# Loading token tile 1 in two halves on two queues, and moving one statistic ahead of an apply

## The chip, the cores and the metric

The kernel runs on one core of one Trainium2 chip. Its time is the device time of one execution in microseconds (us). The core has five engines that run side by side, each with its own list of instructions in a fixed order: TensorE (PE in the profile) multiplies matrices, VectorE (DVE), ScalarE (ACT) and GpSimd (POOL) work on elements, and SyncE (SP) issues most of the transfers between device memory and the on-chip memory. ScalarE issues a few transfers too. An engine waits on semaphores that others raise; matmul results go to PSUM, which has eight banks, and from there they are copied out.

## The reference

One input x of 2048 tokens by 640 features is normalised over its features (mean and variance, no scale), and the result goes through two branches that are added to x:

```
xn = layernorm(x)
A:  q, k, v = split(xn @ wqkv)                # 32 heads of 20
    phi(u) = [softmax(u @ w_phi), softmax(-(u @ w_phi))]   per head
    kv = phi(k)^T v ;  z = sum over tokens of phi(k)
    o = (phi(q) kv) / (phi(q) z + 1e-6)
    a = o @ wo
B:  b = (silu(xn @ w1) * (xn @ w3)) @ w2      # 640 -> 1536 -> 640
out = x + a + b
```

All tensors in memory are bfloat16.

## The kernel before

The 2048 tokens are 16 tiles of 128. Each tile of x is loaded with tokens on partitions (`x_tok`), normalised there, and transposed to features on partitions (`xnT`), 5 chunks of 128 features. Tiles 0 to 3 are transposed by TensorE (`xn_transpose`, L514), tiles 4 to 15 by transposing transfers. From `xnT` TensorE computes v (`v_part`, L559: five matmuls of 512 columns and five of 128 for a tile), the folded k and q projections, and the gated block (`mlp`, L681) in blocks of 512 tokens, so that the first gated block needs all of tiles 0 to 3.

The whole program is built by a list scheduler in Python. `P.op` and `P.dma` describe an operation with its reads, writes and an assumed cost; about a dozen generators (`norms`, `transposes`, `attention`, `mlps` and others, from L735) each yield their next step; the loop at L943 takes the step that, by the assumed costs, can start first, with ties broken by the generators' order. `commit` (L172) books it on its engine. For a load, `commit` adds its bytes, over an assumed rate, to one common bus, and takes a completion time from that. Afterwards `emit` (L212) turns the booked order into one instruction list for each engine, with waits where a dependency crosses engines. So a change in one step can change the order of later ones.

The start of the program is in `first_loads` (L414) and `norms` (L735). `first_loads` issues the loads in this order. On SP: the first half of tile 0 (columns 0 to 319), tile 1, tile 2, the last 128 columns of the v weights `wv`, tile 3, the first third of w1 and w3, `phi_s`, and later ones. On ScalarE's queue: the second half of tile 0, chunks 0 to 2 of the first 512 columns of `wv`, then chunks 3 and 4. The first v matmuls of a tile take chunk 0, 1, 2, 3, 4 in this order.

`norms` orders the normalisation. Tiles 0, 2 and 3 get their statistics on VectorE: two instructions, one for each half of the features (`ln_half`, L455), an aggregate, and a power on GpSimd for the reciprocal standard deviation (`ln_rstd`, L459); then `ln_apply` (L493) normalises the tile in place on VectorE. Tile 1's statistics are taken by ScalarE instead: `act_sum` (L470) twice over the whole tile, a sum for the mean and a sum of squares, then `act_rstd` (L482) with one small VectorE instruction and one on GpSimd. ScalarE's list at the start is therefore: its transfers, the load of its function table and a warm-up, the two sums of tile 1, then its two copies of tile 0's transposes from PSUM to `xnT` (`PARTS`, L511), and so on. For tile 0, VectorE copies chunks 0 and 1, ScalarE chunks 2, 3 and 4.

`transposes` (L800) lets tile 1's transposes go only after the five wide v matmuls of tile 0; `norms` yields `ln_apply(2)` only after tile 1's transposes are booked. `attention` (L820) issues 39 warm-up matmuls, the v parts of tiles 0 to 3 with their copies out of PSUM by ScalarE (`v_store`, L563), and then the k and v projections. After tile 3 `norms` yields a VectorE memset of the ones that stand beside v in `v2` (L758), which v's copies of tiles 2 and 3 must follow, and `block_diag` (L523) on GpSimd, which waits for `phi_s`.

Of the kernel before, what the change touches and what calls it, by code (L numbers as in the profile page):

```python
# [3 lines left out]
ACT = mybir.ActivationFunctionType  # L4
# [5 lines left out]
D = 640  # L10
# [239 lines left out]
def bass_parallel_sum__linear_kernel_hedgehog__glu_gated_swiglu__prompt_kernel(  # L250
# [16 lines left out]
    P = _Program(nc)  # L267
# [12 lines left out]
    def new(name, shape, dtype, offset=None):  # L280
        size = mybir.dt.size(dtype)
        for n in shape[1:]:
            size *= n
        return P.sbuf(name, shape, dtype, region(size) if offset is None else offset)
# [22 lines left out]
    x_tok = new("x_tok", [128, T, D], bf, RX)  # L307
# [83 lines left out]
    def memset(eng, o, v):  # L391
        P.op(eng, "memset", [o], [], (o, v), cost=0.15 + free(o) / 960)
# [7 lines left out]
    x_t = A_x.rearrange("b (t p) d -> p (b t) d", p=128)  # L400
# [6 lines left out]
    def w13(a, b):  # L407
        P.dma("SP", w1_s[:, :, a:b], w1_t[:, :, a:b])
        P.dma("SP", w3_s[:, :, a:b], w3_t[:, :, a:b])

    def load_x(a, b):
        P.dma("SP", x_tok[:, a:b, :], x_t[:, a:b, :])

    def first_loads():  # L414
        def part_wv(eng, i, j, a, b):
            P.dma(eng, wv[:, i:j, a:b], wqkv_t[:, i:j, 2 * D + a:2 * D + b])

        P.dma("SP", x_tok[:, 0, 0:320], x_t[:, 0, 0:320])
        P.dma("ACT", x_tok[:, 0, 320:D], x_t[:, 0, 320:D])
        load_x(1, 2)  # L420
        load_x(2, 3)
        part_wv("ACT", 0, 3, 0, 512)
        part_wv("ACT", 3, DC, 0, 512)
        part_wv("SP", 0, DC, 512, D)
        load_x(3, 4)
        w13(0, 512)
        P.dma("SP", phi_s[:], phi_t)
        P.dma("SP", wqkT[:, DC:2 * DC, :], A_wqkv[:, D:2 * D], True)
        load_x(4, 8)
        load_x(8, 12)  # L430
        load_x(12, 16)
        P.dma("SP", wqkT[:, 0:DC, :], A_wqkv[:, 0:D], True)


    def consts():
        memset("DVE", t1[:, 2, 0:128], 0.0)
        memset("DVE", warm[:], 0.0)
        memset("DVE", bst[:, :, 12:14], 0.0)
        memset("DVE", bst[:, :, 14:15], D * EPS)
        act(warm[:], warm[:], ACT.Exp)  # L440
        memset("POOL", ident[:], 0.0)
        select(ident[:], 0, [[-1, 128]], 1, ALU.not_equal, 1.0)
        memset("POOL", GM[:], 1.0)
        select(GM[:], 0, [[128, DC], [-DH, H]], 1, ALU.is_ge, 0.0)
        select(GM[:], DH, [[-128, DC], [DH, H]], -1, ALU.is_gt, 0.0)
        memset("POOL", mhalf[:], -0.5)
        memset("POOL", M3[:, 0:3], 1.0)
        select(M3[:, 0:3], 0, [[-40, 3]], 1, ALU.is_ge, 0.0)
        select(M3[:, 0:3], 40, [[40, 3]], -1, ALU.is_gt, 0.0)
        memset("POOL", ekt[:, T * 2 * D:T * 2 * D + 48], 1.0)  # L450

    def v_heads(a):
        return a.rearrange("p (g x) -> p g x", x=64)[:, :, 0:63].rearrange("p g (h c) -> p g h c", c=21)

    def ln_half(t, q):  # L455
        i, o = x_tok[:, t, 320 * q:320 * q + 320], bst[:, t, 6 * q:6 * q + 6]
        P.op("DVE", "bn_stats", [o], [i], (o, i), cost=0.48)

    def ln_rstd(t0, n):  # L459
        for t in range(t0, t0 + n):  # L460
            o, i = mv[:, t, 0:2], bst[:, t, 0:15]
            P.op("DVE", "bn_aggr", [o], [i], (o, i), cost=0.22)
        m, v, r, z = mv[:, t0:t0 + n, 0], mv[:, t0:t0 + n, 1], rstd[:, t0:t0 + n, 0], rstd[:, t0:t0 + n, 1]
        P.op("POOL", "tensor_tensor", [r], [v, mhalf[:, 0:n]], (r, v, mhalf[:, 0:n], ALU.pow),
             cost=0.57 if t0 < 4 else 0.73)
        if t0 >= 4:
            P.op("POOL", "tensor_scalar_mul", [z], [m], (z, m, -1.0), cost=0.25)
            P.op("POOL", "tensor_tensor", [z], [z, r], (z, z, r, ALU.mult), cost=0.25)

    def act_sum(t, f, o, bias=None, scale=1.0):  # L470
        j = t1[:].rearrange("p n c -> p (n c)")[:, 0:D]
        i = x_tok[:, t, :]
        kw = dict(accum_out=o, scale=scale)
        if bias is not None:
            kw["bias"] = bias
        P.op("ACT", "activation", [j, o], [i] + ([] if bias is None else [bias]), (j, i, f), kw, cost=0.75)
# [5 lines left out]
    def act_rstd(t):  # L482
        scalar_op(t, rstd[:, t, 0:1], mv[:, t, 1:2], 1.0 / D, EPS)
        r = rstd[:, t, 0:1]
        P.op("POOL", "tensor_tensor", [r], [r, mhalf[:, 0:1]], (r, r, mhalf[:, 0:1], ALU.pow), cost=0.57)

    def ln_stats(t0, n):
        for t in range(t0, t0 + n):
            ln_half(t, 0)
            ln_half(t, 1)  # L490
        ln_rstd(t0, n)

    def ln_apply(t, a=0, b=D):  # L493
        o, m, s, z = x_tok[:, t, a:b], mv[:, t, 0:1], rstd[:, t, 0:1], rstd[:, t, 1:2]
        if t < 4 or P.free["DVE"] < P.free["ACT"] + 0.45:
            P.op("DVE", "tensor_scalar", [o], [o, m, s],
                 (o, o, m, s, ALU.add if t == 1 else ALU.subtract, ALU.mult),
                 cost=0.06 + (b - a) / 1880)
        else:
            P.op("ACT", "activation", [o], [o, s, z], (o, o, ACT.Identity), dict(bias=z, scale=s),  # L500
                 cost=0.9)
# [232 lines left out]

    def norms():  # L735
        yield lambda: (first_loads(), consts())
        yield lambda: act_sum(1, ACT.Copy, mv[:, 1, 0:1], scale=-1.0 / D)
        yield lambda: (ln_half(0, 0), ln_half(0, 1), ln_rstd(0, 1))
        yield lambda: act_sum(1, ACT.Square, mv[:, 1, 1:2], mv[:, 1, 0:1])
        yield lambda: (ln_apply(0, 0, 256), ln_apply(0, 256, D))  # L740
        done["ln"] = 1
        while done["t"] < 1:
            yield None
        yield lambda: act_rstd(1)
        yield lambda: (ln_half(2, 0), ln_half(2, 1))
        yield lambda: ln_apply(1)
        done["ln"] = 2
        yield lambda: ln_rstd(2, 1)
        while done["t"] < 2:
            yield None  # L750
        yield lambda: ln_apply(2)
        done["ln"] = 3
        yield lambda: (ln_half(3, 0), ln_half(3, 1), ln_rstd(3, 1))
        yield lambda: ln_apply(3)
        done["ln"] = 4
        while done["t"] < 4:
            yield None
        yield lambda: memset("DVE", v_heads(v2[:].rearrange("p t n -> p (t n)"))[:, :, :, DH], 1.0)  # L758
        yield block_diag
        done["bd"] = 1  # L760
        todo = []
        for t in range(4, T + 2, 2):
            if t == T or t > done["k"] + 8:
                for u in todo:
                    yield lambda u=u: ln_apply(u)
                    done["ln"] = u + 1
                todo = []
            if t == T:
                break
            while t > done["k"] + 8:  # L770
                yield None
            yield lambda t=t: ln_stats(t, 2)
            for u in todo:
                yield lambda u=u: ln_apply(u)
                done["ln"] = u + 1
            todo = [t, t + 1]
# [153 lines left out]
    def outs():  # L930
        for t in range(T):
            while done["o"] <= t or done["h"] <= t // 4:
# [4 lines left out]
    URGENT = {0: 4.0, 4: 4.0}  # L937
    PROMPT = (6, 8, 10, 11)
    streams = [norms(), transposes(), fold_k(), attention(), k_norms(), loads(), key_values(),
               q_toks(), q_norms(), queries(), q_transposes(), o_transposes(), mlps(), outs()]  # L940
    n = len(streams)
# [100 lines left out]
```

## Time and profile before

| what | us |
|---|---|
| median of 3 runs | 268.19 (268.18 to 268.28) |
| time of the profiled execution | 268.84 |
| its span | 267.1 |
| TensorE busy | 262.7 (98%) |
| VectorE busy | 167.2 (63%) |
| ScalarE busy | 100.8 (38%) |
| GpSimd busy | 99.2 (37%) |
| TensorE's share of the chain that ended last | 96% |

The span reaches from the first to the last instruction of the profiled execution; the execution's time has 1.7 us around it. The clock granted to TensorE is full in every slice of the page. A row of a timeline has the start in us from the span's start, the length of the group, the engine and line, the operation, and what is written from what, with shapes and a count; in brackets stands how long the engine was idle before it and what ended that. Nearly all operations have line 102, the helper that records them, so rows are told apart by their tiles. A matmul's end is modelled, so the starts say more than the lengths.

### The profile page before, as it was taken

To read this page: it belongs to the slowest core of one execution; us is meant where nothing else is said; L and a number is where in the kernel's file an instruction comes from. 1 tells how busy PE (TensorE), PEld (TensorE's weight loads), DVE (VectorE), ACT (ScalarE), POOL (GpSimd) and SP (SyncE) were. 2 spreads that over 40 slices of the span, in tenths; PEclk is the share of its full clock that TensorE was granted. 3 is DMA by queue.
4 is the path that set the end of the run, shared out by engine and by line. 5 is a ranking of instruction groups with operands and counts; after the bars stand their busy time and mean duration, and the time that the engine had idled before them with its cause. 6 is when DMAs were issued, how large, how long until landed. Compare 5 with 4: busy or idle time off the path is not lost.

```text
span 267.1 us, 4841 instructions
## 1 busy us (share of the span) xinstructions
PE 262.7 (98%) x1975; PEld 160.5 (60%) x1975; DVE 167.2 (63%) x289; ACT 100.8 (38%) x200; POOL 99.2 (37%) x137
## 2 busy tenths in 40 slices
PE   8899999999999999999999999999999999999996
PEld 6455777777654555555555445544577777777773
DVE  3659999997467888888889877888512121212112
ACT  4568999988323444443433344322100000000000
POOL 4403699999953544455535334420000000000000
PEclk9999999999999999999999999999999999999999
DMA  7996891870570573374333333213212213131211
GB/s 215 309 324 140 134 239 34 134 253 2 166 234 2 110 97 85 80 93 91 79 81 79 80 81 79 54 28 79 49 52 74 77 50 97 52 97 50 89 37 49
DMA packets 63526, 27.73 MB, mean 104 GB/s; under 512 B 50576, under 2 KB 63504, under 8 KB 63504
## 3 DMA queue, kind: packets, MB, share of 16 engines
q1 hardware_dynamic: 62544, 26.66, 41.4%
q10 hardware_dynamic: 960, 0.77, 0.9%
q8 instruction: 15, 0.25, 0.4%
q14 instruction: 7, 0.06, 0.1%
HBM read 12.81 MB, written 2.62 MB: 58 GB/s over the span
## 4 chain that ended last, share of the span: by engine, by line
PE 96%; DMA 1%; DVE 1%; ACT 1%; SPq 0%; issue 0%
PE PS L102 96%; DMA x_tok<-in_A_x_dram 1%; ACT t L102 1%; DVE bst L102 0%; SPq L114 0%; DVE x_tok L102 0%; DVE xnT L102 0%; DVE xres L102 0%; DVE rstd L102 0%
## 5 line engine op out<-in xcount | busy, mean ns | idle before, releaser
L102 PE MATMUL PS<-xnT,w_s 128*128 128x512 bf16 x480 | 107.5, 379 | 0.1
L102 PEld LDWEIGHTS PS<-xnT,w_s 128*128 128x128 bf16 x480 | 45.8, 98 | 51.2 <-ACT xnT L102 0.3
L102 PE MATMUL PS<-w_s,hT 128*128 128x320 bf16 (+2 forms) x384 | 54.9, 299 | 0.0
L102 DVE TENSOR_TENSOR xres<-PS,xres 128x640 bf16<-128x640 f32 (+2 forms) x17 | 13.4, 786 | 59.8 <-PE PS L102 59.8
L102 ACT ACTIVATE th<-PS 128x512 f32<-128x512 f32 x48 | 29.1, 607 | 45.8 <-PE PS L102 45.8
L102 PEld LDWEIGHTS PS<-w_s,hT 128*128 128x128 bf16 x384 | 37.1, 98 | 15.1
L102 DVE SCALAR_TENSOR_TENSOR t<-th,PS 128x512 bf16<-128x512 f32 x48 | 32.7, 681 | 20.0 <-ACT th L102 19.2
L102 POOL TENSOR_TENSOR ekt<-ekt,rS 128x640 bf16<-128x640 bf16 x32 | 39.6, 1271 | 1.7 <-DVE rS L102 1.7
L102 ACT ACTIVATE eq<-PS 128x600 bf16<-128x600 f32 (+1 forms) x72 | 23.9, 418 | 33.8 <-PE PS L102 33.8
L102 DVE SCALAR_TENSOR_TENSOR hT<-t,PS 128x512 bf16<-128x512 bf16 x48 | 33.0, 688 | 5.4 <-DVE t L102 0.5
L102 PE MATMUL PS<-wv,xnT 128*128 128x320 bf16 (+2 forms) x160 | 24.8, 299 | 0.6 <-ACT xnT L102 0.6
L102 PE MATMUL PS<-wo_s,oT 128*128 128x320 bf16 (+2 forms) x160 | 24.5, 299 | 0.0
L102 PE MATMUL PS<-Wqp,xnT 128*128 128x512 bf16 (+1 forms) x160 | 24.3, 299 | 0.0
L102 PE MATMUL PS<-Wkp,xnT 128*128 128x320 bf16 x160 | 23.7, 299 | 0.0
L102 POOL TENSOR_TENSOR rq<-rq,Sq 128x32 f32<-128x32 f32 x16 | 4.1, 255 | 52.5 <-DVE rq L102 52.5
L102 DVE TENSOR_REDUCE S<-ekt 128x64 f32<-128x1280 bf16 x16 | 23.0, 1436 | 0.2 <-ACT ekt L102 0.2
L102 POOL TENSOR_TENSOR eq<-eq,rq 128x600 bf16<-128x600 bf16 (+1 forms) x32 | 22.7, 730 | 1.2
L102 POOL TENSOR_TENSOR half<-eq 128x660 f32<-128x660 bf16 x15 | 20.4, 1359 | 4.5 <-ACT eq L102 4.5
L102 ACT ACTIVATE ekt<-PS 128x640 bf16<-128x640 f32 x32 | 20.8, 733 | 2.3 <-PE PS L102 2.3
L102 PEld LDWEIGHTS PS<-wv,xnT 128*128 128x128 bf16 x160 | 14.8, 98 | 8.0 <-ACT xnT L102 1.3
L102 PEld LDWEIGHTS PS<-wo_s,oT 128*128 128x128 bf16 x160 | 15.5, 98 | 6.5
L102 PEld LDWEIGHTS PS<-Wkp,xnT 128*128 128x128 bf16 x160 | 15.4, 98 | 6.1 <-ACT v L102 0.2
(57 smaller groups left out, 177.1 us busy)
## 6 DMA issues: line engine op xcount, KB each, us to landing
w_s<-in_B_w_dram SPq DMA_DIRECT2D x6, 640.0 KB, 5.7
xres<-in_A_x_dram SPq DMA_DIRECT2D x16, 160.0 KB, 2.5
out_dram<-xres SPq DMA_DIRECT2D x15, 160.0 KB, 1.8
x_tok<-in_A_x_dram SPq DMA_DIRECT2D x3, 640.0 KB, 6.0
w_s<-in_B_w_dram SPq DMA_DIRECT2D x1, 1920.0 KB, 7.4
wo_s<-in_A_wo_dram SPq DMA_DIRECT2D x1, 800.0 KB, 6.8
x_tok<-in_A_x_dram SPq DMA_DIRECT2D x3, 160.0 KB, 4.5
wv<-in_A_wqkv_dram ACTq DMA_DIRECT2D x1, 384.0 KB, 4.6
```

Of the source, the lines that this page charges most:

```text
L102: o = _Op(eng, lambda: m(*args, **kw), r, w, cost)
```

## The change

In `first_loads`, the load of tile 1 as one transfer of 128 rows of 1280 bytes on SP becomes two of 640 bytes: columns 0 to 319 on SP, and columns 320 to 639 on ScalarE's queue. Both are issued directly after the halves of tile 0, and so ScalarE's part stands ahead of the two transfers of `wv` that ScalarE issues. The number of transfers on SP stays as it was; ScalarE issues one more. The transfers that follow keep their order on each queue.

In `norms`, the first of tile 3's two statistics instructions is yielded ahead of `ln_apply(2)` instead of after it; the second, the aggregate and the power stay after it.

```diff
         P.dma("SP", x_tok[:, 0, 0:320], x_t[:, 0, 0:320])
         P.dma("ACT", x_tok[:, 0, 320:D], x_t[:, 0, 320:D])
-        load_x(1, 2)
+        P.dma("SP", x_tok[:, 1, 0:320], x_t[:, 1, 0:320])
+        P.dma("ACT", x_tok[:, 1, 320:D], x_t[:, 1, 320:D])
         load_x(2, 3)
         part_wv("ACT", 0, 3, 0, 512)
         part_wv("ACT", 3, DC, 0, 512)
...
         while done["t"] < 2:
             yield None
+        yield lambda: ln_half(3, 0)
         yield lambda: ln_apply(2)
         done["ln"] = 3
-        yield lambda: (ln_half(3, 0), ln_half(3, 1), ln_rstd(3, 1))
+        yield lambda: (ln_half(3, 1), ln_rstd(3, 1))
         yield lambda: ln_apply(3)
```

## The prediction

> **What bounds the kernel now.** I read the chain that ended last first, in order of time, because it says which stage a saving must come from. Its columns are start, length, and what ran.
>
> ```profile
> 1.25 3.78 DMA x_tok<-in_A_x_dram
> ...
> 5.05 0.84 ACT t L102 x2
> ...
> 5.92 0.93 ACT t L102 x2
> ...
> 6.87 0.15 DVE rstd L102
> ...
> 8.22 3.85 PE PS L102 x34
> ...
> 12.44 33.79 PE PS L102 x246
> ...
> 46.26 218.54 PE PS L102 x1640
> ```
>
> From 12.44 us to the end TensorE is the chain, and it waits for almost nothing there. So only time before 12.44 can be won, plus whatever a new plan breaks later. Before 8.22 the chain is tile 1's normalisation: its load lands at 5.03 (1.25 + 3.78), then ScalarE's two sums, then rstd, the apply and TensorE's transposes. Next I read TensorE's timeline in that stretch.
>
> ```profile
> 5.29 0.63 PE L102 MATMUL PS<-ident,x_tok 128*128 128x128 bf16 x5
> 5.96 0.60 PE L102 MATMUL PS<-wv,xnT 128*128 128x512 bf16 x2
> 7.16 0.82 PE L102 MATMUL PS<-wv,xnT 128*128 128x512 bf16 x3 [0.60 <-ACT xnT L102]
> 8.22 0.45 PE L102 MATMUL PS<-ident,x_tok 128*128 128x128 bf16 x5 [0.24 <-DVE x_tok L102]
> ...
> 9.55 0.44 PE L102 MATMUL PS<-ident,x_tok 128*128 128x128 bf16 x5
> 9.83 2.06 PE L102 MATMUL PS<-wv,xnT 128*128 128x512 bf16 x14
> 11.77 0.45 PE L102 MATMUL PS<-ident,x_tok 128*128 128x128 bf16 x5
> 12.05 0.33 PE L102 MATMUL PS<-wv,xnT 128*128 128x128 bf16 x3
> 12.44 2.33 PE L102 MATMUL PS<-xnT,w_s 128*128 128x512 bf16 x10
> 14.61 1.52 PE L102 MATMUL PS<-wv,xnT 128*128 128x512 bf16 x10
> ```
>
> The four rows of five are the transposes of tiles 0 to 3. Ten 512-column matmuls take 14.61 - 12.44 = 2.17, so one costs 0.22; a tile's ten v matmuls take about 1.36 (to 15.96, where the next row starts), so its five 128-column ones cost 1.36 - 5 x 0.22 = 0.26. Five transposes take 9.83 - 9.55 = 0.28. Between 5.29 and 12.44 stand four sets of transposes (1.1) and three tiles of v (4.1): 5.2 us of work in 7.15. Some 2 us are bubbles, the two largest with their releasers in brackets. The first waits for ScalarE's copies of tile 0, which are queued behind its two sums of tile 1; the second waits for tile 1's apply. One late load makes both.
>
> Then the loads, by the views of issues in narrow windows (last figure: us from issue to landing), with the two queues' issue times.
>
> ```profile
> x_tok<-in_A_x_dram ACTq DMA_DIRECT2D x1, 80.0 KB, 2.4
> x_tok<-in_A_x_dram SPq DMA_DIRECT2D x1, 160.0 KB, 3.8
> wv<-in_A_wqkv_dram ACTq DMA_DIRECT2D x1, 384.0 KB, 4.6
> ...
> x_tok<-in_A_x_dram SPq DMA_DIRECT2D x1, 160.0 KB, 4.5
> wv<-in_A_wqkv_dram ACTq DMA_DIRECT2D x1, 256.0 KB, 5.1
> ...
> wv<-in_A_wqkv_dram SPq DMA_DIRECT2D x1, 160.0 KB, 5.3
> x_tok<-in_A_x_dram SPq DMA_DIRECT2D x1, 160.0 KB, 5.2
> ```
>
> ```profile
> 0.81 1.33 SPq L114 DMA_DIRECT2D x_tok<-in_A_x_dram  x3
> 0.81 0.40 ACTq L114 DMA_DIRECT2D x_tok<-in_A_x_dram  x1
> 1.25 0.99 ACTq L114 DMA_DIRECT2D wv<-in_A_wqkv_dram  x2
> 2.18 0.43 SPq L114 DMA_DIRECT2D wv<-in_A_wqkv_dram  x1
> 2.66 0.52 SPq L114 DMA_DIRECT2D x_tok<-in_A_x_dram  x1
> ```
>
> With issues about 0.46 apart, these land at: tile 0 by 3.2, tile 1 at 5.0, wv chunks 0-2 at 5.85, tile 2 at 6.2, wv chunks 3-4 at 6.85, wv's last columns at 7.5, tile 3 at 7.9. That is nearly the order of issue, with landings set by the bytes ahead: 704 KB by 5.85, 864 by 6.2, 1120 by 6.85, 1280 by 7.5.
>
> **The change part by part.** *Tile 1 in halves.* One more issue on ScalarE's queue, none more on SP's. Queued behind it are the two wv issues, the table load and the sums.
>
> ```profile
> 2.27 1.28 ACT L102 ACT_TABLE_LOAD   x1 [2.27 <-issue]
> 3.56 0.21 ACT L102 ACTIVATE warm<-warm 128x8 f32<-128x8 f32 x1
> 5.05 0.74 ACT L102 ACTIVATE t<-x_tok 128x640 bf16<-128x640 bf16 x1 [1.28 <-DMA x_tok<-in_A_x_dram]
> ...
> 6.74 0.53 ACT L102 ACTIVATE xnT<-PS 128x256 bf16<-128x256 bf16 x2
> ```
>
> The issue costs ScalarE about 0.46, so the table load moves to 2.7 and ScalarE is free at 3.77 + 0.46 = 4.2; the 1.28 of idle time covers it. Tile 1's landing: at the earliest its 160 KB behind tile 0 at 250 GB/s (last column of the row by stretches below, from 2 to 3 us), 3.2 + 0.65 = 3.9; at the latest the old 5.0. Both halves now stand ahead of every wv byte, so I take the near end, about 4.1. Then ScalarE's own queue is the limit: the sums start at 4.24, 0.81 earlier. The whole chain behind them follows: squares done 6.03, copies of tile 0 at 5.93, rstd to VectorE at 6.06, apply(1) ending at about 7.35 instead of 8.16, transposes possible at 7.41.
>
> ```profile
> 2.00:3.00 1.00, 1.00 (x12) 1.00 (x11) 0.00 (x0) 0.73 (x1) 0.79 (x6) 1.00 1.01 250
> ```
>
> What is late next is wv. On its queue it now has 80 KB more ahead, and against it on SP's queue stands tile 2 instead of tile 1. If the order of issue holds, with SP's first of each pair as before, chunks 0-2 have 864 KB behind them when done instead of 704, so they land between 5.85 and 6.2; chunks 3-4 between 6.85 and 7.5 (1280 KB). Chunk 3 is the fourth matmul of tile 0, chunk 4 the fifth, and the transposes of tile 1 come after those in TensorE's order. I take 7.2, the middle. Then the fourth matmul starts at 7.25, and tile 1's transposes at 7.25 + 2 x 0.22 = 7.7 instead of 8.22: 0.53 won (0.28 for a landing at 7.5; 0.81 for 6.85, where the apply at 7.41 is the limit).
>
> [...]
>
> *Tile 3's first statistic ahead of apply(2).* VectorE's order changes from copy(1), apply(2), two statistics to copy(1), statistic, apply(2), statistic.
>
> ```profile
> 8.54 0.29 DVE L102 COPY xnT<-PS 128x256 bf16<-128x256 bf16 x1 [0.25 <-PE PS L102]
> 8.96 0.45 DVE L102 TENSOR_SCALAR x_tok<-x_tok,mv,rstd 128x640 bf16<-128x640 bf16 x1
> 9.32 1.01 DVE L102 BATCH_NORM_STATS2 bst<-x_tok 128x6 f32<-128x320 bf16 x2
> ...
> 11.26 0.45 DVE L102 TENSOR_SCALAR x_tok<-x_tok,mv,rstd 128x640 bf16<-128x640 bf16 x1 [0.66 <-POOL rstd L102]
> ...
> 14.23 0.50 DVE L102 MEMSET v<- 128x528 bf16 x1 [1.85 <-issue]
> ```
>
> It was free while apply(2) waited from 8.83 to 8.96 for rstd. After part one that wait is gone (rstd(2) comes 0.8 earlier, copy(1) only 0.53), so a statistic's 0.4 to 0.5 is paid in full: apply(2) starts at about 8.7 instead of a possible 8.3. TensorE meanwhile has tile 1's v matmuls. By the planner's costs tile 2's transposes lose their tie and one more such matmul goes ahead of them; they start near 9.25, TensorE idle for nothing. Their copy on ScalarE ends near 10.1, and tile 2's v then waits about 0.14. Tile 3's second statistic, aggregate, rstd and apply all move up: apply(3) at about 10.5 instead of 11.26, 0.2 of it from this part. TensorE then reaches the end of tile 2's v with tile 3 ready, and the pause there, from three matmuls of 0.05 at 12.05 (done 12.22) to 12.44, goes: 0.22 won.
>
> **The sum** goes by the profiled run: span 267.1, time 268.84, against a median of 268.19, so 0.65 above. Won: 0.53 + 0.22 - 0.14 = 0.61, with 0.03 of a smaller pause ahead of 11.77: 0.64. The profile would show a span of 266.5, the median 268.19 - 0.64 = 267.55. By the ends of wv's landing it is 0.4 to 0.9: 267.8 to 267.3. After 12.44 I cost everything at nothing: the runs of 33.79 and 218.54 us in the chain show TensorE never short of data there. They do not show by what margin, and the planner will place some of that work anew; that stands in the third rival and in the range.
>
> **The rivals.** *One: the split brings nothing.* If tile 1 still lands at 5.0, ScalarE's sums stay where they are, and wv at 7.2 only meets the 7.16 at which chunk 2 was multiplied anyway. Then the statistic delays apply(2) by 0.28 (copy ends 8.83, plus 0.41, against 8.96), which the one matmul ahead covers; tile 3 comes 0.2 earlier, and some 0.1 is won: 268.1. [...] Against: tile 1 and wv were issued together at 1.25, and wv's 384 KB were its competitors. [...]
>
> *Two: wv eats the gain.* If chunks 3-4 land at 7.7 or later, tile 1's transposes start at 8.2 as before; 0.1 is left, 268.1. For it: the 256-byte rows of wv's last columns compete with them, and 80 KB pieces may move worse. Against: the bytes ahead of them are 1280 KB at most, which landed at 7.5.
>
> *Three, slower: ScalarE's order turns.* With tile 3 ready sooner the planner sees tile 2's v copy free before the first gate-up block's second weight, puts v of tiles 2 and 3 ahead of that block, and so both v copies ahead of its tanh. A v copy must wait for VectorE's memset of v's ones, which ended at 14.73, and that stood behind GpSimd:
>
> ```profile
> 11.72 1.97 POOL L102 TENSOR_TENSOR BDc<-phi_s,GM 128x140 bf16<-128x140 bf16 x5 [0.50 <-DMA phi_s<-in_A_w_phi_dram]
> ```
>
> It started only after these products, done at 13.69 and released by a load whose time does not move. Then the copies take 14.77 to 16.1 and the tanh comes at 16.1 instead of 13.72, and the block's banks open 2.4 later. If TensorE needs them, it stalls by up to 2.4. The result turns slower by 0.2% once that stall passes 0.64 + 0.54 = 1.2; with a stall of 1.6 it is 269.1. For it: the memset row's 1.85 idle. Against: TensorE has four pairs of banks and its next blocks use the others; and if tile 3's copy ends before 11.7, the memset goes first.
>
> **How the numbers follow.** I give the forecast 0.62, rivals one and two 0.18 together, rival three 0.20. The limit for telling a change, 0.2%, is 0.54 us here, and my 0.64 is just past it: of the forecast's 0.62 about 0.12 fall short of it. So faster 0.50, same 0.12 + 0.18 = 0.30, slower 0.20. The likeliest is 267.55. The range takes the good end of wv's landing with 0.15 for bubbles I did not see, 267.15, and reaches over the first two rivals into the third, 268.6.
>
> **What would show it.** Right: the first sum near 4.2; wv's chunks landing near 6.2 and 7.2; tile 1's transposes near 7.7, with TensorE's 0.60 wait then on a load; a statistic between copy(1) and apply(2); tile 3's apply near 10.5; the 33.79 and 218.54 runs of the chain still unbroken and shifted by 0.6. Wrong: a sum still at 5.05 (rival one), transposes of tile 1 at 8.2 behind wv (two), or new TensorE idle time after 13 us released by ScalarE's tanh or VectorE (three).

## The result, and the profile after

The changed kernel takes 268.98 us (median of 14 executions, 268.68 to 270.62), the kernel before 268.29 in the same comparison (14 executions, 268.09 to 269.04). The ratio is 1.004, 95% interval 1.0023 to 1.0057: slower by 0.4%, where 267.55 was predicted. Nine of the 14 lie between 268.68 and 269.20 with a granted clock of 1.0 (median 268.89, 0.6 above before); five lie between 270.03 and 270.62, and four of these show a mean granted clock of 0.994. The profiled execution below is one of those (270.4, span 268.7), so that both losses can be seen in it.

The load that was made earlier is earlier. These are rows of the changed kernel's timeline, first ScalarE, then VectorE.

```profile
4.17 0.72 ACT L102 ACTIVATE t<-x_tok 128x640 bf16<-128x640 bf16 x1
...
6.83 0.43 DVE L102 TENSOR_SCALAR x_tok<-x_tok,mv,rstd 128x640 bf16<-128x640 bf16 x1
...
9.38 0.48 DVE L102 BATCH_NORM_STATS2 bst<-x_tok 128x6 f32<-128x320 bf16 x1
9.78 0.43 DVE L102 TENSOR_SCALAR x_tok<-x_tok,mv,rstd 128x640 bf16<-128x640 bf16 x1
```

Tile 1's first sum starts at 4.17 with no wait (4.24 was predicted), its apply at 6.83. But TensorE, in the same view, does not get to tile 1's transposes before 8.72:

```profile
5.20 0.63 PE L102 MATMUL PS<-ident,x_tok 128*128 128x128 bf16 x5
6.70 0.81 PE L102 MATMUL PS<-wv,xnT 128*128 128x512 bf16 x3 [0.88 <-DMA wv<-in_A_wqkv_dram]
7.91 1.02 PE L102 MATMUL PS<-wv,xnT 128*128 128x512 bf16 x2 [0.40 <-DMA wv<-in_A_wqkv_dram]
8.72 0.74 PE L102 MATMUL PS<-ident,x_tok 128*128 128x128 bf16 x5
9.25 0.74 PE L102 MATMUL PS<-wv,xnT 128*128 128x128 bf16 x5
10.21 1.40 PE L102 MATMUL PS<-wv,xnT 128*128 128x512 bf16 x3 [0.22 <-DVE x_tok L102]
```

It waits twice for `wv`, 0.88 for chunks 0 to 2 and 0.40 for chunks 3 and 4. The chain that ended last says the same (start, length, what ran):

```profile
1.25 0.46 ACTq L114
1.73 0.46 ACTq L114
2.21 5.65 DMA wv<-in_A_wqkv_dram
7.86 0.05 issue
7.91 1.24 PE PS L102 x4
```

Tile 1's normalisation, the head of the chain before, is gone from it; the load of chunks 3 and 4, issued at 2.21 as ScalarE's fourth transfer and landed at 7.86, stands in its place.

Then look at the matmuls' lengths: five transposes take 0.74 here and took 0.45 before. The view by stretches of the changed kernel has the reason (the stretch and its length, busy time and in brackets the count for PE, PEld, DVE, ACT, POOL, then granted clock, DMA share and GB/s):

```profile
5.00:6.00 1.00, 0.68 (x6) 0.28 (x5) 0.75 (x4) 0.99 (x3) 0.00 (x0) 1.00 1.00 298
6.00:7.00 1.00, 0.30 (x2) 0.21 (x3) 1.00 (x4) 0.37 (x2) 0.56 (x1) 1.00 1.01 332
7.00:8.00 1.00, 0.60 (x4) 0.11 (x3) 0.40 (x2) 0.00 (x0) 0.53 (x1) 0.98 1.08 356
8.00:9.00 1.00, 1.00 (x5) 0.45 (x5) 0.00 (x0) 0.00 (x0) 0.02 (x1) 0.50 1.09 383
9.00:10.00 1.00, 0.99 (x10) 0.94 (x9) 0.82 (x3) 0.49 (x1) 0.00 (x0) 0.50 1.09 387
10.00:11.00 1.00, 0.79 (x2) 0.30 (x2) 0.84 (x3) 0.72 (x1) 0.05 (x1) 0.50 1.58 291
11.00:12.00 1.00, 1.00 (x10) 0.59 (x9) 0.45 (x1) 0.19 (x1) 0.50 (x1) 0.81 1.01 105
```

TensorE was busy for 0.68, 0.30 and 0.60 of three microseconds, and then its clock was granted at half: (0.02 + 0.5 x 3 + 0.19) / 0.5 = 3.42 us of it. Such an execution is about 1.5 us longer (270.4 against 268.89); half of 3.42, 1.71, is the most that the halved clock can have taken. Not every long execution is of this kind: the one of 270.03 has a full clock, and no run shows what made it long.

### The profile page after: what moved, and what is told of

Its sections match the earlier page's. It is cut to its first block, busy times and chain, and to the rows that moved or that the text cites. A ratio compares the mean times of both kernels' runs of the same rounds, so it can differ in the third digit from the quotient of the medians.

```text
span 268.7 us, 4822 instructions
## 1 busy us (share of the span) xinstructions
PE 262.5 (98%) x1954; PEld 161.2 (60%) x1975; DVE 167.2 (62%) x289; ACT 100.5 (37%) x200; POOL 99.2 (37%) x137
## 4 chain that ended last, share of the span: by engine, by line
PE 95%; DMA 2%; issue 1%; DVE 0%; ACTq 0%
PE PS L102 95%; DMA wv<-in_A_wqkv_dram 2%; ACTq L114 0%; DVE bst L102 0%; DVE x_tok L102 0%; DVE xres L102 0%; DVE xnT L102 0%
## 5 line engine op out<-in xcount | busy, mean ns | idle before, releaser
L102 PE MATMUL PS<-xnT,w_s 128*128 128x512 bf16 x466 | 105.6, 379 | 0.7
L102 PE MATMUL PS<-wv,xnT 128*128 128x320 bf16 (+2 forms) x159 | 25.9, 309 | 1.5 <-DMA wv<-in_A_wqkv_dram 1.3
L102 PE MATMUL PS<-Wqp,xnT 128*128 128x512 bf16 (+1 forms) x155 | 23.3, 296 | 0.3
```

Source lines behind the costliest of these rows:

```text
L102: o = _Op(eng, lambda: m(*args, **kw), r, w, cost)
```

## The experiments

Four questions: what is the kernel before really like at its start, which part of the change costs, through what, and can the loss be taken away while tile 1 stays early.

**The kernel before, once more.** No edit.

> The kernel before, unchanged. Theory A (my profile of before was of an execution in which tile 1's load came late): the median stays near 268.2, and a profile whose span is 1.7 below a time near 268.2, that is about 266.5, shows tile 1 landing near 4.2 instead of 5.03 and TensorE's waits of 0.60 and 0.24 before 8.3 us shrunk by about 0.6 together. Theory B (that profile was typical, and 0.65 above the median is only the profiler's cost): the same 5.03 and the same waits with a span near 267.1.

Measured: 268.33 (268.05 to 268.58), ratio 1.0 (0.9991 to 1.0009). Its profiled execution took 268.13, that of the prediction 268.84. Rows of its loads (last figure: us to landing; tile 1 was issued at 1.27, wv's chunks 0 to 2 at 1.24, chunks 3 and 4 at 1.73):

```profile
x_tok<-in_A_x_dram SPq DMA_DIRECT2D x1, 160.0 KB, 3.1
...
wv<-in_A_wqkv_dram ACTq DMA_DIRECT2D x1, 384.0 KB, 4.2
...
wv<-in_A_wqkv_dram ACTq DMA_DIRECT2D x1, 256.0 KB, 4.8
```

And of its timeline, TensorE's rows:

```profile
6.06 1.25 PE L102 MATMUL PS<-wv,xnT 128*128 128x512 bf16 x5
7.51 0.45 PE L102 MATMUL PS<-ident,x_tok 128*128 128x128 bf16 x5 [0.20 <-DVE x_tok L102]
...
11.73 2.33 PE L102 MATMUL PS<-xnT,w_s 128*128 128x512 bf16 x10
```

Tile 1 lands at 4.32 and its first sum starts at 4.35, not at 5.05; the five wide matmuls of v run unbroken and tile 1's transposes stand at 7.51, not at 8.22. The execution from which the prediction was made was 0.7 longer than this one, and most of that was this one load. So this execution had 4.35 - 4.17 = 0.18 to win at ScalarE, not 0.81. The run with the statistic alone (below) has the same loads; in its profiled execution (268.26) tile 1 landed at 4.56 and the sum started at 4.58, which leaves 0.41.

**Each part alone.** The split without the moved statistic, and the statistic without the split:

```diff
-        load_x(1, 2)
+        P.dma("SP", x_tok[:, 1, 0:320], x_t[:, 1, 0:320])
+        P.dma("ACT", x_tok[:, 1, 320:D], x_t[:, 1, 320:D])
```

> The split load alone; the statistic stays where it was, and so does the order on every engine. Theory W (the loss comes from the v weights landing later, at about 6.6 and 7.9 instead of 5.85 and 6.85, so that TensorE waits for them): about 268.9 where the clock holds, with single executions near 270.3 in which the granted clock is halved for 3.4 us. Theory P (the loss comes from the new order that the moved statistic brings): 268.0 or less, no execution near 270.

```diff
...
+        yield lambda: ln_half(3, 0)
         yield lambda: ln_apply(2)
         done["ln"] = 3
-        yield lambda: (ln_half(3, 0), ln_half(3, 1), ln_rstd(3, 1))
+        yield lambda: (ln_half(3, 1), ln_rstd(3, 1))
```

> The moved statistic alone; the loads are those of before, the order on TensorE, ScalarE and VectorE is that of the changed kernel. Theory W: no loss, 267.9 to 268.3, no execution near 270. Theory P: the loss of the changed kernel, about 268.9, with tile 2's apply late and ScalarE's tanh behind the two copies of v.

Measured: the split alone 268.93 (268.43 to 270.75), ratio 1.0032 (1.0015 to 1.0048), three of 12 executions above 270.3 with a clock of 0.994. The statistic alone 268.20 (268.00 to 268.82), ratio 0.9996 (0.9987 to 1.0004), clock 1.0 throughout. The loss is the split's. With the split alone all engines keep their order of computing, so it owes nothing to the planner. Its profiled execution has a full clock (span 267.2), and TensorE's rows there show the first loss by itself:

```profile
7.08 1.45 PE L102 MATMUL PS<-wv,xnT 128*128 128x512 bf16 x5 [1.17 <-DMA wv<-in_A_wqkv_dram]
8.37 0.44 PE L102 MATMUL PS<-ident,x_tok 128*128 128x128 bf16 x5
...
12.53 2.33 PE L102 MATMUL PS<-xnT,w_s 128*128 128x512 bf16 x10
```

The first gated block starts at 12.53 against 11.73, 0.8 later, and so is the span (267.2 against 266.4). In the run with the statistic alone ScalarE's order turned as the third rival had it; rows of its timeline, of TensorE and ScalarE:

```profile
13.21 4.05 PE L102 MATMUL PS<-xnT,w_s 128*128 128x512 bf16 x17
...
14.14 1.33 ACT L102 ACTIVATE v<-PS 128x660 bf16<-128x660 f32 x2 [2.09 <-DVE v L102]
15.35 0.60 ACT L102 ACTIVATE th<-PS 128x512 f32<-128x512 f32 x1
```

Both v copies wait for the memset, 2.09, and the tanh comes at 15.35. TensorE runs its gated block over all of it without a pause, and the time does not move: the chain of events was real and free.

**Why is wv late?** Between 3.5 and 4.0 us something is missing. Stretches of the kernel before (the repeated run), then of the split alone; the last figure is GB/s:

```profile
3.00:3.50 0.50, 0.50 (x8) 0.50 (x6) 0.46 (x2) 0.50 (x1) 0.25 (x2) 1.00 0.85 262
3.50:4.00 0.50, 0.50 (x7) 0.50 (x6) 0.47 (x3) 0.27 (x2) 0.00 (x0) 1.00 1.04 310
4.00:4.50 0.50, 0.50 (x8) 0.50 (x6) 0.19 (x1) 0.15 (x1) 0.23 (x1) 1.00 1.09 353
```

```profile
3.00:3.50 0.50, 0.50 (x8) 0.50 (x6) 0.45 (x2) 0.50 (x1) 0.25 (x2) 1.00 1.42 188
3.50:4.00 0.50, 0.50 (x7) 0.50 (x6) 0.47 (x3) 0.50 (x1) 0.00 (x0) 1.00 0.62 80
4.00:4.50 0.50, 0.50 (x8) 0.50 (x6) 0.20 (x1) 0.49 (x3) 0.22 (x1) 1.00 0.87 239
...
6.00:7.00 1.00, 0.00 (x0) 0.00 (x0) 1.00 (x4) 0.45 (x2) 0.56 (x1) 1.00 1.12 352
```

The kernel before moves 0.5 x (262 + 310 + 353) = 462 KB there, the split alone 253. The missing 209 KB are 0.59 us at the later 352 GB/s. The kernel before has 704 KB issued in its first two slots (tile 0, tile 1, chunks 0 to 2 of wv); with the halves it has 320 KB, and both 384 KB of wv and tile 2 are issued at 1.73. I read it as the loads running dry before those get going. The changed kernel's profile, with the same loads, shows less of it: 226 GB/s from 3.0 to 4.5, so 339 KB. Rows of the split alone, of the two transfers issued at 1.73:

```profile
wv<-in_A_wqkv_dram ACTq DMA_DIRECT2D x1, 384.0 KB, 5.2
x_tok<-in_A_x_dram SPq DMA_DIRECT2D x1, 160.0 KB, 3.9
```

Tile 2 landed at 5.60 and wv's chunks 0 to 2 at 6.95. Five runs test what in the split does this.

*The later issue alone.* Tile 1 stays whole; ScalarE issues 4 KB of another tile ahead of wv.

```diff
         load_x(1, 2)
+        P.dma("ACT", x_tok[:, 15, 0:16], x_t[:, 15, 0:16])
```

> The kernel before with a transfer of 4 KB (16 columns of tile 15, loaded again later) issued by ScalarE ahead of wv: the issue of wv comes 0.46 to 0.5 later, with no bytes to speak of ahead of it, and tile 1 stays whole on SP. If the time of issue decides (tile 2, issued at 1.72, then goes ahead of wv, issued at 1.73): chunks 0-2 land at 6.0 to 6.9 instead of 5.5, TensorE waits for them from 5.97 on, tile 1's transposes move from 7.5 to about 7.9, and the time is 268.5 to 268.9. If the 80 KB of tile 1's half decide: chunks 0-2 land by 5.6, and the time is that of before, 268.3.

Measured: 269.02 (268.38 to 270.90), ratio 1.0039 (1.0017 to 1.0062). One more issue on ScalarE's queue, with next to no bytes, costs about as much as the split by the ratios. Without the long executions it costs somewhat less: seven of the 12 lie between 268.38 and 269.03 (median 268.66, 0.4 above before), five between 270.11 and 270.90, three of them with a clock of 0.994; of the split alone, the nine below 269.2 have a median of 268.89 (0.5 above). The profiled execution (the best, 268.38) has wv's chunks 0 to 2 issued at 1.73 and landed at 6.16, tile 2 ahead of them at 5.38, and 219 GB/s between 3.0 and 4.5. It also shows that tile 1 needs no halves to be early. This is the row of tile 1, whole and on SP:

```profile
x_tok<-in_A_x_dram SPq DMA_DIRECT2D x1, 160.0 KB, 2.4
```

It landed at 3.65, as early as the two halves of the split alone (3.50 and 3.68), where wv's 384 KB are issued behind it; with them issued beside it, as in the kernel before, it landed at 4.32 and 5.03. Tile 1 early and wv late come from the same thing.

*Both halves on SP*, so that wv keeps its issue at 1.24; once without and once with the moved statistic. (One charge in the planner's bookkeeping was left out to keep the order of computing.)

```diff
-        load_x(1, 2)
+        P.dma("SP", x_tok[:, 1, 0:320], x_t[:, 1, 0:320])
+        P.dma("SP", x_tok[:, 1, 320:D], x_t[:, 1, 320:D])
```

> Tile 1 in two halves, both on SP's queue and one behind the other; ScalarE issues what it issued before, and every engine keeps the order of before (in the planner's books the extra issue takes no time). Theory Q (the v weights come late because ScalarE's queue issues them 0.5 later and with 80 KB ahead, so that tile 2's load passes them): wv chunks 0-2 land near 5.5 as in the kernel before, no wait of TensorE for wv, 268.2 to 268.4, granted clock 1.000 throughout. Theory H (the halves themselves, with rows of 640 bytes, move worse): wv late again, 268.6 or more. Either way tile 1 lands no earlier than 4.2, since the whole load already landed at 4.3.

> Both halves on SP and the statistic moved: ScalarE's queue as before, the order of the other engines that of the changed kernel. If the loss of the change is only wv on ScalarE's queue: 268.1 to 268.3, not slower than before, with no wait for wv and the clock at 1.000. If the new order loses by itself once tile 1 is early: 268.6 or more.

Measured: 269.46 (269.18 to 269.95), ratio 1.0047 (1.0034 to 1.0060), and 270.00 (269.13 to 271.00), ratio 1.0065 (1.0043 to 1.0086), three of the second's six executions with a clock of 0.994. The times agree with the second reading of each expectation (268.6 or more), but the reasons given there do not hold. There is no hole (307 and 298 GB/s from 3.0 to 4.5), but the second half, now in SP's third slot at 1.72, landed at 5.37 and 6.06, and the sum waited for it. Chunks 0 to 2 of wv, issued at 1.24, landed at 4.99 in the first, in time, and at 6.24 in the second, where TensorE waited 0.26 for them: the issue time alone does not fix the landing.

*The second half on GpSimd's queue*, so that the pieces stay and wv has its issue time; without and with the statistic.

```diff
-        load_x(1, 2)
+        P.dma("SP", x_tok[:, 1, 0:320], x_t[:, 1, 0:320])
+        P.dma("POOL", x_tok[:, 1, 320:D], x_t[:, 1, 320:D])
```

> The split alone, but tile 1's second half issued by GpSimd, ahead of its first memset, so that ScalarE's queue is as in the kernel before and wv's chunks 0-2 are issued at 1.25 again. If the loss comes from the hole in the loads between 3.0 and 4.5 us (253 KB moved there in the run with the split alone, 462 KB in the kernel before), because only 320 KB are issued before 1.7: 430 KB or more move there again, the five wide matmuls of v run unbroken from about 6.0, and the time is 267.9 to 268.4. If small pieces are bad by themselves: the hole stays and the time is 268.9. If GpSimd's transfer starts late (nothing in the trace of before shows one), tile 1's first sum waits for it beyond 4.35 and the time is above 268.4 by that delay, with wv in time.

> The changed kernel with only the queue of tile 1's second half changed, from ScalarE's to GpSimd's. By the hole: 267.7 to 268.4, no granted clock under 1.0, first sum between 3.8 and 4.4, wv's chunks 0-2 landing by 5.9. By small pieces: 268.9 as the changed kernel.

Measured: 270.48 (269.32 to 271.44, five of six with a clock of 0.994), ratio 1.0080 (1.0067 to 1.0093), and 269.57 (269.14 to 270.53), ratio 1.0051 (1.0035 to 1.0067). For the first of the two, the row of the stretch from 3.0 to 4.5:

```profile
3.00:4.50 1.50, 1.50 (x17) 1.50 (x15) 1.11 (x3) 0.77 (x2) 1.22 (x8) 1.00 0.94 313
```

Two rows of its loads, SP's half of tile 1 and GpSimd's:

```profile
x_tok<-in_A_x_dram SPq DMA_DIRECT2D x1, 80.0 KB, 3.0
x_tok<-in_A_x_dram POOLq DMA_DIRECT2D x1, 80.0 KB, 4.1
```

And ScalarE's first sum in its timeline:

```profile
5.45 0.74 ACT L102 ACTIVATE t<-x_tok 128x640 bf16<-128x640 bf16 x1 [1.68 <-DMA x_tok<-in_A_x_dram]
```

The hole is gone, 313 GB/s, with the same small pieces: it belongs to wv's late issue, not to the pieces. The time does not profit, because the half issued by GpSimd at 1.32 needed 4.1 us to land (4.6 in the other run), where SP's half, issued at 1.26, needed 3.0 (2.8): tile 1 was late, the third case of the first expectation. The issue also kept GpSimd busy for 0.78 us ahead of its other work, and tile 0's transposes start at 5.55 instead of 5.28. In the second run, two of whose six executions have a clock of 0.994, wv's chunks 0 to 2 landed at 6.33 in spite of their issue at 1.26, which its expectation (by 5.9) did not have.

Over all profiles of this case the rate from 3.0 to 4.5 us falls into two groups: 269 to 313 GB/s in seven profiles with wv's chunks 0 to 2 issued at 1.25, 120 to 234 in ten with that issue at 1.73.

**wv ahead of tile 2.** SP issues wv's wide transfers directly behind its half of tile 1, so that tile 2 can't pass them: both of them; chunks 0 to 2 alone; both with the moved statistic. The diff of the first:

```diff
-        load_x(1, 2)
+        P.dma("SP", x_tok[:, 1, 0:320], x_t[:, 1, 0:320])
+        P.dma("ACT", x_tok[:, 1, 320:D], x_t[:, 1, 320:D])
+        part_wv("SP", 0, 3, 0, 512)
+        part_wv("SP", 3, DC, 0, 512)
         load_x(2, 3)
-        part_wv("ACT", 0, 3, 0, 512)
-        part_wv("ACT", 3, DC, 0, 512)
```

> Tile 1 in halves as in the change, statistic not moved, and both wide transfers of wv issued by SP behind tile 1 and ahead of tile 2's load, so that nothing but tiles 0 and 1 stands ahead of them; ScalarE issues the halves of tiles 0 and 1 only. If the loss comes from tile 2's load passing wv: chunks 0-2 have 704 KB done with them as in the kernel before and land at 5.5 to 5.9, chunks 3-4 near 6.6, no wait of TensorE for wv above 0.4, tile 1's first sum near 3.8, its transposes at 7.2 to 7.5, and a time of 267.9 to 268.4 (tile 2, issued 0.9 later, may cost back what tile 1 wins). If the halves on two queues are bad by themselves (smaller rows, more descriptors), the wide wv lands near 6.9 and 7.9 as with the split alone and the time is 268.9 again.

> As the run beside it, but only wv's chunks 0-2 go to SP, ahead of tile 2; chunks 3-4 stay with ScalarE, now its third transfer, issued at the same 1.72. Chunks 0-2 and 3-4 are then issued together with 960 KB in front of the later of them: chunks 0-2 land between 5.9 and 6.6, chunks 3-4 at 6.6 to 6.9, tile 2 behind them near 7. Time 267.9 to 268.5 if wv being passed by tile 2 is the cause, 268.9 if the halves are.

> Both parts of the change, with both wide transfers of wv issued by SP ahead of tile 2. If the moved statistic is worth nothing and wv's lateness was the whole loss, the time is that of the same kernel without the moved statistic within 0.3 us (267.9 to 268.4); if the two parts harm each other, it is above 268.7 though wv lands early.

Measured: 269.25 (268.65 to 269.75), ratio 1.0028 (1.0019 to 1.0037); 270.43 (268.80 to 272.32), ratio 1.0072 (1.0041 to 1.0103); 269.17 (268.67 to 271.06), ratio 1.0037 (1.0020 to 1.0054). All three are slower, and the times expected were missed. In the first, wv was in time and something else was not; its timeline, TensorE and VectorE:

```profile
6.05 1.37 PE L102 MATMUL PS<-wv,xnT 128*128 128x512 bf16 x5
...
6.64 0.89 DVE L102 BATCH_NORM_STATS2 bst<-x_tok 128x6 f32<-128x320 bf16 x2 [0.58 <-DMA x_tok<-in_A_x_dram]
7.44 0.43 DVE L102 TENSOR_SCALAR x_tok<-x_tok,mv,rstd 128x640 bf16<-128x640 bf16 x1
...
7.93 0.45 PE L102 MATMUL PS<-ident,x_tok 128*128 128x128 bf16 x5 [0.52 <-DVE x_tok L102]
```

The five matmuls are unbroken from 6.05, as before. Now tile 2, issued at 2.7, lands behind wv (6.6), VectorE takes its statistics ahead of tile 1's apply, and the apply waits behind them until 7.44. In the run with chunks 0 to 2 alone the two wide transfers of wv were issued at the same 1.73, the rate from 3.0 to 4.5 was 120 GB/s, the lowest of all, and the first wide matmul came at 7.49. That expectation (268.9 at most) missed by 1.5.

*Tile 1's apply ahead of tile 2's statistics*, on top of it, without and with the moved statistic:

```diff
-        yield lambda: (ln_half(2, 0), ln_half(2, 1))
         yield lambda: ln_apply(1)
         done["ln"] = 2
-        yield lambda: ln_rstd(2, 1)
+        yield lambda: (ln_half(2, 0), ln_half(2, 1), ln_rstd(2, 1))
```

> Tile 1 in halves, both wide transfers of wv on SP ahead of tile 2 (as in the run before it, where wv was in time and the loss stood in VectorE's queue), and now VectorE applies tile 1 before it takes tile 2's statistics; tile 3's statistic not moved. If the loss there was the apply of tile 1 standing behind tile 2's late load: the apply ends near 7.0, tile 1's transposes start at 7.3 (behind the five wide matmuls of v) instead of 7.93, the first gated block near 11.9 instead of 12.43, and the time is 268.0 to 268.6. If tile 2's lateness is the limit whatever the order (its apply near 8.8, tile 3's near 11.1), the first gated block stays near 12.4 and the time near 269.2.

> The same with tile 3's first statistic ahead of tile 2's apply. Here the statistic has a wait to fill (tile 2's power on GpSimd, which now ends last before its apply), so it should bring tile 3's apply to about 10.7, and the time to 267.7 to 268.4; if it is again worth nothing, the same as the run beside it within 0.3.

Measured: 269.38 (268.93 to 270.22), ratio 1.0039 (1.0025 to 1.0052); 269.47 (268.86 to 270.14), ratio 1.0044 (1.0030 to 1.0057). No gain. The first one's profiled execution, a long one (270.22), shows the apply at 6.75 as meant, and then these rows of TensorE's:

```profile
6.58 1.24 PE L102 MATMUL PS<-wv,xnT 128*128 128x512 bf16 x5 [0.56 <-DMA wv<-in_A_wqkv_dram]
...
9.47 1.32 PE L102 MATMUL PS<-wv,xnT 128*128 128x128 bf16 x9 [1.37 <-DMA wv<-in_A_wqkv_dram]
```

wv's last 128 columns, issued at 3.23, landed at 9.4. Each order of these loads found another one to be late. How far that is the order and how far the executions' own spread isn't settled. In the four kernels with this list of loads wv's chunks 0 to 2, issued at 1.73 with tile 2 behind them, landed at 5.55, 5.66, 6.45 and 6.69 in their one profile each, and tile 2, issued at 2.7, at 6.61, 6.75, 7.55 and 7.74. In the last two TensorE waited 0.56 and 0.90 for wv although tile 2 could not pass it: tile 2's place is not the whole of wv's lateness.

**The clock.** Idle matmuls (of zeros, results unused, as in the warm-up) were put where TensorE waited for wv: 13 ahead of the first wide matmul and 9 ahead of the fourth in the changed kernel; 13 in the one with the split alone (its diff; `filler` issues that many of them).

```diff
...
-    yield lambda t=t, q=q, i=i, k=k: v_part(t, q, i, k)
+    f = 13 if (t, q, i) == (0, 0, 0) else 0
+    yield lambda t=t, q=q, i=i, k=k, f=f: (filler(f), v_part(t, q, i, k))
```

> The changed kernel with 13 idle 128-column matmuls ahead of the first v matmul and 9 ahead of the fourth, where TensorE waits for the v weights; nothing else moves. If the executions near 270.3 come from the clock falling after TensorE's idle time: none of them is left, the granted clock is 1.000 in all, and the median stays at the clean 268.8 to 268.9 (the waits themselves remain). If they come from something else (a late load): they stay as frequent as in the changed kernel, 5 of 14.

> The split load alone, with 13 idle 128-column matmuls (0.7 us) between tile 0's transposes and its first v matmul, where TensorE waited 1.17 us for wv; the 9 at the second place are left out. If TensorE's idle time is what halves the clock in 3 of 12 executions: none of 10 or more, and the median stays at 268.9. If the clock falls for another reason: again a quarter of the executions near 270.4.

Measured: 269.48 (268.90 to 270.04, six executions), ratio 1.0043 (1.0027 to 1.0059), and 268.96 (268.15 to 269.24), ratio 1.0023 (1.0015 to 1.0032). In all 18 executions the clock was 1.0, where the changed kernel had 0.994 in four of 14 and the split alone in three of 12. So it is TensorE's idle time that brings the clock down in some of the executions, and filling it prevented that here. The second kernel still takes 0.7 more than before: that is the wait for wv itself. In the first the idle matmuls stood in the way (tile 1's transposes at 8.79).

## Why the prediction was wrong

**"The sum goes by the profiled run: span 267.1, time 268.84, against a median of 268.19, so 0.65 above."** This step failed first. The prediction noted the 0.65, took the whole gain off the median all the same, and never asked where the 0.65 stood in the trace. It stood in tile 1's load, the very thing to be improved: landed at 5.03 there, at 4.32 in the repeated run of 268.13, and at 4.56 in the run with the statistic alone (268.26). The 0.81 at ScalarE was 0.18 and 0.41 in these two. The 0.53 at tile 1's transposes was 0.20 and 0.43 at most, even with wv in time: they came at 7.51 and 7.74, and with the apply at 6.83, as in the changed kernel, and the 0.48 that the repeated run has from the apply's start to the transposes, they could come at 7.31. With the 0.11 of the other terms that is 0.31 to 0.54, an estimate from these profiles, and not 0.64.

**"What is late next is wv"** was the right mechanism, and its size was wrong; this is the step that turned the sign. Chunks 0 to 2 were put between 5.85 and 6.2 and landed at 6.6 (6.95 with the split alone), chunks 3 and 4 at 7.2 and landed at 7.86 (7.88). The rule behind it, landings set by the bytes ahead, took the loads to be running all the time. Tile 2 did pass, 1.35 ahead of chunks 0 to 2 with the split alone (5.60 against 6.95) where it was 0.5 behind them before (5.98 against 5.48), but the prediction had that in its 864 KB and 6.2. What it left out is the stretch in which little moved, with 320 KB instead of 704 issued by 1.3 us. Its own profile has 281 GB/s from 3.0 to 4.5, 421 KB; the changed kernel has 82 KB less there, the split alone 168 KB less. At 352 GB/s these are 0.23 and 0.48 us, by this estimate some two thirds of the 0.37 and 0.75 by which chunks 0 to 2 came behind 6.2. The rest is not explained. The extra issue was costed at "about 0.46" with "the 1.28 of idle time covers it": so it is for ScalarE's sums, and not for the transfers issued behind it. A small slip besides, on which nothing hangs: with the 0.05 that the sum allows behind a landing, the low end for a landing at 7.5 is 0.23, not 0.28.

**Rival two, "wv eats the gain",** is the one that happened: chunks 3 and 4 beyond its 7.7. Its price was too low since it let tile 1's transposes start at 8.2 "as before"; the repeated run has 7.51, and they came at 8.37 with the split alone. Against it the prediction said that "the bytes ahead of them are 1280 KB at most, which landed at 7.5": that is the same rule, and it fell with it.

**The statistic** was worth 0.1 to 0.2 in the prediction and measured -0.04% (interval -0.13 to +0.04%): nothing that can be told. The row between copy(1) and apply(2) is there (9.38), as predicted, but tile 3's apply came at 11.54, behind wv, not near 10.5.

**Rival three** had its whole chain of events (v copies 2.08 late in the changed kernel, 2.09 with the statistic alone) and its decisive point, a stall of TensorE, did not occur. The reason given against it, that TensorE's next blocks use the other banks, agrees with its unbroken 4.05 us row.

**The clock** was in no rival. The prediction costed TensorE's waits at their length; in about a quarter of the executions they cost another 1.5 us. The length of one wait does not decide it in these profiles: in the changed kernel's the waits from 5 to 8 us were 0.88 and 0.40, and the clock stood at half for 3.42 us behind them; in that of the split alone one wait of 1.17 left the clock full. What makes it fall in one execution and not in the next was not shown.

**The second queue** by itself brought nothing in the landings: tile 1 whole, on SP, landed at 3.65 in the 4 KB run, where the halves on two queues landed at 3.50 and 3.68 with the split alone. The later issue of wv that came with it did cost: with its 384 KB issued 0.48 us later, the time was 0.4 us longer in the executions below 269.1 and 0.8 longer by the medians (the 4 KB run, 268.66 and 269.02 against 268.24).

Two losses, then: about 0.4 to 0.7 us from the late wv in the usual execution, shown by the split alone (0.5), by the 4 KB transfer (0.4) and by the filled kernel (0.7); and 1.5 us in about a quarter of them from the clock, shown by the filled kernels. No tried version beats the kernel before; the statistic alone is level with it. Open is why less was moved at the start where fewer bytes stood in the first two slots (226 and 169 GB/s from 3.0 to 4.5 with 320 KB, 281 and 308 with 704), how the empty stretch and the order of the landings share the lateness of wv, what lengthens the few long executions at a full clock, and whether an order of loads exists that brings tile 1 to 3.7 and costs nothing.

## What to carry to other kernels

Before a late event in a profile is counted as a gain, compare the profiled execution's time with the median of the runs; if it is longer, look first whether the excess is that very event. At a start that waits for loads, a transfer issued ahead of a large one can delay it even with few bytes (here 4 KB ahead of 384: issue 0.48 later, landing 6.16 instead of 5.48, in one profile each): count what is issued in the first slots, and ask which load becomes the last one. A new wait of TensorE is not priced by its length alone: look at the granted clock behind it (here half of full speed for 3.42 us behind waits of 0.88 and 0.40, and full behind one of 1.17).

## What the runs showed of the hardware that was not expected

- A hole in the loads: with 320 KB issued by 1.3 us and the next 544 KB at 1.73, the rate fell to 80 GB/s between 3.5 and 4.0 us with the split alone (220 in the changed kernel), where 310 were moved with 704 KB issued by 1.3.
- The clock was granted at half for 3.42 us after three microseconds in which TensorE was busy for 0.53 on average; three more of the 14 executions have the same mean clock of 0.994.
- 80 KB issued by GpSimd took 4.1 and 4.6 us to land, beside 3.0 and 2.8 for the other 80 KB of the same tile, issued by SP 0.05 earlier. The difference at the landing was 1.1 and 1.8. GpSimd's issue took 0.78, ScalarE's of 80 KB 0.40 and 0.41 in the same two profiles; what makes up the rest was not shown.
- One load's landing varies by 0.7 us and more between executions of the same list of loads: tile 1 at 4.32, 4.56 and 5.03 with the loads of before, wv's chunks 0 to 2 at 5.55 to 6.69 in the four kernels that issue them ahead of tile 2.
